# Column-tiled matmuls of linear attention gathered into every second step

## The chip, the cores and the metric

The program runs on one core of one Trainium2 chip. Time is device microseconds of one execution; a kernel's figure is the median of its runs. One more execution is recorded by the hardware profiler, and all rows below come from it. The engines are TensorE (PE, its weight loads as PEld), VectorE (DVE), ScalarE (ACT), GpSimd (POOL) and SyncE (SP), which issues most of the DMAs. Each engine works through its own instructions in order; a semaphore holds an instruction until what it needs is done.

## The reference

Linear attention over 8 batches of 8 heads, 576 tokens and 64 dimensions, then a mixture of 8 experts with one expert per token, and a second MLP:

```python
def phi(x):
    proj = np.einsum('bhsd,df->bhsf', x, w_phi)          # 64 -> 128 features
    proj = proj - np.max(np.abs(proj), axis=-1, keepdims=True)
    return np.concatenate([np.exp(proj), np.exp(-proj)], axis=-1)
q_p, k_p = (phi(q), phi(k))
kv = np.einsum('bhsf,bhsd->bhfd', k_p, v)
z = np.sum(k_p, axis=2)
num = np.einsum('bhsf,bhfd->bhsd', q_p, kv)
den = np.einsum('bhsf,bhf->bhs', q_p, z)[..., None] + 1e-06
attn = num / den
...
e_idx = np.argmax(logits, axis=1)                        # logits = x @ w_gate + bias of the modality
out[mask] = gate_w[mask, None] * (relu(x[mask] @ w1[e]) @ w2[e])
...
h = x @ w_in                                             # softmax times h, layer norm, then @ w_out
```

## The kernel before

Only attention is touched, the first third of the program. A unit (`ui`, 0 to 7) is two batches and four heads; the batches are its two halves. Its tokens are nine jobs `i`: 0 to 3 in half 0, 4 with a rest of both halves, 5 to 8 in half 1. A **step** `st` does one k job and one q job. The loop over the steps writes TensorE's order by hand (`manual_schedule`); the orders of the other engines follow from a timeline that the framework keeps while the program is built.

In step `st` TensorE gets, one behind the other:

- four transposes of k and q for the next step (`s0`, L255); ScalarE copies them into `hi` (L258), VectorE writes the remainder `lo` (L259);
- the projection of k, six matmuls (L267 to L269) into a bank `mm`; VectorE takes the largest absolute value (L271) and subtracts it (L273), and ScalarE writes the exponentials `e` (L277, L278);
- four transposes of the q features of the step two before (L330), which ScalarE turns into `qp` (L338), and an item of the list "f";
- the projection of q, in the same way, and up to two items "f";
- the sums over keys and values of the k job of two steps before (`accum_kv`, L283), four matmuls with 64 columns, into the bank `kv`. GpSimd adds the same `e` into `es` (L322);
- up to two items of the list "64": value groups (`num_part`, L440), 64 columns; and one of the list "32": row sums (`den_part`, L454) or sums of keys (`z_sum`, L384), 32 columns.

After jobs 4 and 8 `finish_kv` is called: ScalarE copies `kv` into `kt` (L325), and the items of that half are put on the lists: `kf_part` (L399, copied by L403 and L407), `z_part` (L416), four value groups, two row sums, and `finish`, which transposes the results back (L545, L560; VectorE L549 to L551 and L562) and, in odd units, does the gating (L575 to L626). An item runs when those before it are done.

PSUM has eight banks: three `tp` for transposes, four `mm` for projections, value groups, row sums and sums of keys, and one `kv`:

```python
tps = ctx.enter_context(tc.tile_pool(name="a_tp", bufs=3, space=PSUM))
mmp = ctx.enter_context(tc.tile_pool(name="a_mm", bufs=4, space=PSUM))
kvp = ctx.enter_context(tc.tile_pool(name="a_kv", bufs=1, space=PSUM))
```

In unit 5 the gating of the last part ends with `early.pick`: it finds the largest expert so far and writes its number into `ea_tab` (L845 to L857). In step 63 + `PRE` `prefetch` puts the loads of that expert's weights on SP's queue; they wait for `ea_tab` (issue at L884). In step 63 + `STEP0` `split_raw` cuts the first of these weights in two, with a cast on ScalarE (L926) and a subtraction on VectorE (L927), which write `w64`. L658 is the first matmul that reads prefetched weights.

Of the kernel before, what the change touches and what calls it, by code (L numbers as in the profile page):

```python
# [39 lines left out]
COLS64 = 2  # L40
COLS32 = 1
# [1 line left out]
BIAS = 8  # L43
BGN = 1
BGP = 100
PRE = 2
FSTEP = 2
RING = 5
RING0 = 1
# [144 lines left out]
def attention(ctx, tc, c, cnt, xe, q, k, v, ld, early, m, late):  # L194
# [86 lines left out]
    def accum_kv(u, i, e):  # L281
        def mm(half, h, lhsT, rhs, first, last):
            T.matmul(  # L283
                u.kv[half][(h % 2) * D : (h % 2 + 1) * D, h // 2, :], lhsT=lhsT, rhs=rhs,
                start=first, stop=last, skip_group_check=True,
            )

        def begin(half):
            u.kv[half] = kvp.tile([P, 2, 2 * F], F32, name="kv")
            u.es[half] = w2p.tile([P, 4, 2, F], F32, name="es")  # L290
            G.memset(u.es[half], 0.0)

        def rest(half, e, first, last):
            rows = slice(half * D, (half + 1) * D)
            es = u.es[half]
            for h in range(4):
                mm(half, h, u.src["v", 2][rows, h, :], e[rows, h], first and h < 2, last)
            G.tensor_tensor(out=es[rows], in0=es[rows], in1=e[rows], op=ALU.add)

        if i == 4:  # L300
            rest(0, e, False, True)
            u.erest = e
        else:
            half = i // 5
            if i in (0, 5):
                begin(half)
            if i == 5:
                rest(1, u.erest, True, False)
            rp, hp = (i - half) // 2 % 2, (i - half) % 2
            vt = u.src["v", half]  # L310
            for r in range(2):
                for h2 in range(2):
                    h = 2 * hp + h2
                    mm(
                        half, h, vt[:, h, (2 * rp + r) * D : (2 * rp + r + 1) * D], e[:, 2 * h2 + r],
                        i == 0 and r == 0, i == 8,
                    )
            es = u.es[half]
            ev = e.rearrange("p (h r) a f -> p h r (a f)", r=2)
            eo = es[:, 2 * hp : 2 * hp + 2].rearrange("p h a f -> p h (a f)")  # L320
            for r in range(2):
                G.tensor_tensor(out=eo, in0=eo, in1=ev[:, :, r, :], op=ALU.add)  # L322
        if i in (4, 8):
            u.kt[i // 5] = w2p.tile([P, 2, 2 * F], F32, name="kt")
            A.copy(u.kt[i // 5], u.kv[i // 5])  # L325
# [32 lines left out]
    def run_items(kind, count):  # L358
        ran = 0
        while ran < count:  # L360
            it = next((x for x in items if x.kind == kind and x.runnable()), None)
            if it is None:
                break
            if isinstance(it, Chain):
                said = next(it.gen, items)
                if said is not items:
                    if said:
                        until = step[0] + said[1]
                        it.kind, it.ready = said[0], lambda: step[0] >= until
                    ran += 1  # L370
                    continue
            else:
                it.fn()
            it.done = True
            items.remove(it)
            ran += 1
        return ran
# [3 lines left out]
    def z_sum(u, half):  # L381
        zp = mmp.tile([P, 2 * F], F32, name="mm")
        for h in range(4):
            T.matmul(  # L384
                zp[32 * h : 32 * h + 32, :], lhsT=c.ones32, rhs=u.es[half][:, h, :, :],
                start=True, stop=True, tile_position=(0, 32 * h), skip_group_check=True,
            )
        zs = w2p.tile([P, 2, F], F32, name="zs")
        A.copy(zs, zp.rearrange("p (a f) -> p a f", a=2))
        u.zs[half] = zs  # L390
# [21 lines left out]
    def z_part(u, half):  # L412
        gdt = gd[(2 * u.g + half) % 2]
        tp = tps.tile([P, 2, P], F32, name="tp")
        for fh in range(2):
            T.transpose(tp[:, fh, :], u.zs[half][:, fh, :], c.ident)  # L416
        A.copy(gdt[:, :, :, E : E + 1], tp.rearrange("p a (h n) -> p a h n", n=32)[:, :, :, 0:1])
# [50 lines left out]
    def finish_kv(u, half):  # L468
        at = step[0]
        zi = Item("32", lambda: z_sum(u, half), ready=lambda: step[0] > at)  # L470
        kfs = [Item("f", lambda j=j: kf_part(u, half, j)) for j in range(2)]
        zt = Item("f", lambda: z_part(u, half), after=[zi])
        begin = Item("0", lambda: outputs(u, half))
        parts = []
        for ci, (_, need) in enumerate(CHUNKS[half]):
            ok = lambda need=need: u.qdone.issuperset(need)
            for j in range(2):
                parts.append(Item("64", lambda ci=ci, j=j: num_part(u, half, ci, j), after=[begin, kfs[j]], ready=ok))
            parts.append(Item("32", lambda ci=ci: den_part(u, half, ci), after=[begin, zt, *kfs], ready=ok))

        def rest():
            yield from finish(u, half, 0, 4)
            if half == 1:
                yield from finish(u, 2, 0, 1)
            if u.g == 1:
                yield "0", 0
                yield from gating(u, 4 * half, 4 + half)
                if u.p2 == 2 and half == 1:
                    early.pick(cnt[0])
                    early.ready = True  # L490

        Chain("f", rest(), after=parts)

    def finish_last(u):
        z_sum(u, 1)
        yield
        for j in range(2):
            kf_part(u, 1, j)
        yield
        z_part(u, 1)  # L500
        yield
        outputs(u, 1)
        for ci in range(2):
            for j in range(2):
                num_part(u, 1, ci, j)
                yield
            den_part(u, 1, ci)
            yield
            if ci == 0:
                yield from finish(u, 2, 0, 1)  # L510
            else:
                yield from pend
            yield from finish(u, 1, 2 * ci, 2)
            if ci == 0:
                pend = gating(u, 4, 3)
                next(pend)
            else:
                pend = gating(u, 7, 2)
                for n in range(2):
                    for _ in range(FSTEP):  # L520
                        next(pend, None)
                    first_slot(n)
                yield from pend
# [142 lines left out]
    def last_unit():  # L666
        return U.get(len(units) - 1)
# [10 lines left out]
    n = len(steps)  # L678
    feats = {}
    bias = late()  # L680
    tail = []
    for st in range(n + LAGF):
        step[0] = st
        if st == 9 * 7 + PRE:
            assert early.ready
            m.prefetch()
        if st == 9 * 7 + STEP0:
            for i in range(RING0):
                m.split_raw(1, i)
        if st == BIAS:  # L690
            bias()
        run_items("0", 4)
        if st + 1 < n:
            ui, jobs = steps[st + 1]
            if ("k", 5) in jobs:
                unit(ui + 1)
            hl[st + 1] = s0(unit(ui), jobs)
        old = feats.pop(st - LAGF, ())
        u_old = unit(steps[st - LAGF][0]) if st >= LAGF else None
        kjobs = [(i, x) for kind, i, x in old if kind == "k"]  # L700
        qjobs = [(i, x) for kind, i, x in old if kind == "q"]
        if st < n:
            h_ = hl.pop(st)
            feats[st] = []
        for a in range(2):
            if st < n:
                kind, i = steps[st][1][a]
                feats[st].append((kind, i, proj(h_, a, kind)))
            if qjobs:
                i, x = qjobs.pop(0)  # L710
                q_features(u_old, i, x)
                u_old.qdone.add(i)
            run_items("f", FSLOT[a])
        for i, x in kjobs:
            accum_kv(u_old, i, x)
            if i in (4, 8):
                if i == 8 and u_old is last_unit():
                    tail.append(finish_last(u_old))
                else:
                    finish_kv(u_old, i // 5)  # L720
        run_items("0", 4)
        run_items("64", COLS64)
        run_items("32", COLS32)
        if st >= n and tail:
            for _ in range(TAIL):
                next(tail[0], None)
# [894 lines left out]
```

## Time and profile before

| what | value |
|---|---|
| median of 3 runs | 1294.19 us (1291.05 to 1295.75) |
| profiled execution | 1293.31 us, of which the span of the trace is 1291.6 us |
| TensorE, VectorE, ScalarE, GpSimd busy | 98%, 67%, 52%, 31% of the span |
| granted TensorE clock, mean | 0.996 of full speed |

The median is what the change is measured by; sums over the trace belong to the profiled execution, 0.88 us under the median. Matmuls overlap and their ends are modelled, so their start times tell more than their busy time. Start times are in us from the start of the span.

### The profile page before, as it was taken

What the parts mean: (1) busy time and instruction counts of PE and PEld (TensorE: products, weight loads), DVE (VectorE), ACT (ScalarE), POOL (GpSimd) and SP (SyncE); (2) the same over time, 40 slices, a digit from 0 to 9 for tenths busy, and PEclk for the clock granted to TensorE, in tenths of its full rate; (3) what the DMA queues carried; (4) which work ended last, traced back from release to release, by engine and by line L of the source; (5) the groups of instructions that cost most, each with busy time, mean ns of one, the idle gap of its engine ahead of it and who ended that gap; (6) DMA issues with size and microseconds to landing.
All of it is one profiled execution on the core that took longest, in us unless ns stands there. A gap on an engine that the chain in (4) does not pass through costs nothing.

```text
span 1291.6 us, 25365 instructions
## 1 busy us (share of the span) xinstructions
PE 1260.4 (98%) x9242; PEld 1057.8 (82%) x9242; DVE 869.3 (67%) x1620; ACT 666.8 (52%) x1254; POOL 403.8 (31%) x479
## 2 busy tenths in 40 slices
PE   8999999999999989999999999999999999999997
PEld 7767777777766889999999999987777778888885
DVE  8757866876775848778878787747555555566562
ACT  5666666666665426555555555534334434444442
POOL 6655674674663200000000000013323323333331
PEclk9999999999999999999999999999999999999999
DMA  8711342232132222222623132477877875566542
GB/s 246 214 54 58 107 133 58 87 117 85 50 116 67 91 67 92 67 83 66 197 66 83 51 83 67 130 213 192 233 204 168 248 169 142 137 153 139 145 121 57
DMA packets 273760, 156.78 MB, mean 121 GB/s; under 512 B 181824, under 2 KB 255712, under 8 KB 273632
## 3 DMA queue, kind: packets, MB, share of 16 engines
q1 hardware_dynamic: 267648, 136.01, 39.3%
q0 software_dynamic: 5824, 19.04, 3.8%
q8 instruction: 75, 1.23, 0.4%
q14 instruction: 53, 0.43, 0.1%
q10 hardware_dynamic: 160, 0.07, 0.0%
HBM read 166.67 MB, written 51.37 MB: 169 GB/s over the span
## 4 chain that ended last, share of the span: by engine, by line
PE 53%; DMA 5%; SPq 2%; issue 1%; ACT 1%; DVE 1%; POOL 0%; POOLq 0%; ACTq 0%; DVEq 0%
PE tp L1078 26%; PE h L1078 25%; DMA turned<-whi 2%; PE tp L898 1%; DMA gd<-xe 1%; SPq L1248 1%; DMA wlo<-turned 1%; PE tp L1389 1%; SPq L884 1%; DMA yin<-yd 0%; ACT ex L1265 0%; DVE ex L1270 0%; DMA xin<-xe 0%; ACT whi L1297 0%; SPq L1228 0%
## 5 line engine op out<-in xcount | busy, mean ns | idle before, releaser
L322 POOL TENSOR_TENSOR es<-es,e 128x512 f32<-128x512 f32 x128 | 163.8, 1286 | 102.5 <-ACT e L278 90.9
L927 POOL TENSOR_TENSOR yTl<-yin,yTh 128x512 fp32r<-128x512 f32 x36 | 46.8, 1300 | 443.2 <-ACT yTh L926 442.1
L1078 PE MATMUL tp<-xTh,whi 128*128 128x256 f32 x432 | 121.7, 282 | 2.5 <-PEq L1470 2.1
L1078 PE MATMUL h<-hTl,whi 128*128 128x256 f32 x432 | 120.6, 279 | 0.4 <-DVE hTl L1093 0.4
L1078 PE MATMUL tp<-xTh,wlo 128*128 128x256 f32 x432 | 120.6, 279 | 0.0
L1078 PE MATMUL tp<-xTl,whi 128*128 128x256 f32 x432 | 120.5, 279 | 0.0
L1078 PE MATMUL h<-hTh,whi 128*128 128x256 f32 x432 | 120.5, 279 | 0.0
L1078 PE MATMUL h<-hTh,wlo 128*128 128x256 f32 x432 | 120.5, 279 | 0.0
L271 DVE TENSOR_REDUCE m<-mm 128x4 f32<-128x512 f32 x144 | 97.1, 681 | 15.9 <-PE mm L269 15.9
L259 DVE TENSOR_TENSOR lo<-tp,hi 128x512 fp32r<-128x512 f32 x72 | 49.6, 689 | 82.5 <-ACT hi L258 82.0
L1265 ACT ACTIVATE ex<-h,s_mx,gt 128x1024 f32<-128x1024 f32 x36 | 43.4, 1207 | 111.6 <-issue 56.8
L1260 DVE TENSOR_REDUCE s_mx<-h 128x1 f32<-128x512 f32 x72 | 46.3, 685 | 80.6 <-PE h L1078 80.6
L267 PE MATMUL mm<-wphi_hi,hi 128*128 128x256 f32 x288 | 94.2, 327 | 1.0 <-ACT hi L258 1.0
L1275 ACT ACTIVATE sq<-ex 128x1024 bf16<-128x1024 f32 x36 | 38.1, 1058 | 97.9 <-DVE ex L1272 97.9
L1078 PEld LDWEIGHTS tp<-xTh,whi 128*128 128x128 f32 x432 | 81.3, 188 | 2.9 <-issue 2.2
L338 ACT ACTIVATE qp<-tp 128x512 f32<-128x512 f32 x128 | 69.3, 597 | 25.8 <-PE tp L330 22.7
L1078 PEld LDWEIGHTS tp<-xTh,wlo 128*128 128x128 f32 x432 | 81.9, 190 | 0.0
L1078 PEld LDWEIGHTS h<-hTh,wlo 128*128 128x128 f32 x432 | 81.9, 190 | 0.0
L268 PE MATMUL mm<-wphi_lo,hi 128*128 128x256 f32 x288 | 81.6, 283 | 0.0
L1078 PEld LDWEIGHTS h<-hTl,whi 128*128 128x128 f32 x432 | 81.1, 188 | 0.6 <-DVE hTl L1093 0.6
L269 PE MATMUL mm<-wphi_hi,lo 128*128 128x256 f32 x288 | 81.4, 283 | 0.0
L1078 PEld LDWEIGHTS h<-hTh,whi 128*128 128x128 f32 x432 | 81.3, 188 | 0.0
(427 smaller groups left out, 3818.9 us busy)
## 6 DMA issues: line engine op xcount, KB each, us to landing
ldk<-in_moe_w_dram SPq DMA_DIRECT2D x66, 512.0 KB
ldv<-in_moe_w_dram SPq DMA_DIRECT2D x66, 512.0 KB
ldq<-in_moe_w_dram SPq DMA_DIRECT2D x44, 512.0 KB
turned<-whi SPq DMA_DIRECT2D x35, 512.0 KB
wlo<-turned SPq DMA_DIRECT2D x140, 128.0 KB
yd<-yo SPq DMA_DIRECT2D x36, 256.0 KB
yin<-yd SPq DMA_DIRECT2D x18, 512.0 KB
xin<-xe SPq DMA_DIRECT2D x16, 512.0 KB
```

The lines of the kernel that those rows point to most:

```text
L259: V.tensor_tensor(out=lo, in0=tp, in1=hi.bitcast(F32), op=ALU.subtract)
L267: T.matmul(o, lhsT=hi[:, 2 * a + j, :], rhs=c.wphi_hi, start=(j == 0), stop=False, skip_group_check=True)
L268: T.matmul(o, lhsT=hi[:, 2 * a + j, :], rhs=c.wphi_lo, start=False, stop=False, skip_group_check=True)
L269: T.matmul(o, lhsT=lo[:, 2 * a + j, :], rhs=c.wphi_hi, start=False, stop=True, skip_group_check=True)
L271: V.tensor_reduce(out=m, in_=pj, axis=AX.X, op=ALU.max, apply_absolute_value=True)
L322: G.tensor_tensor(out=eo, in0=eo, in1=ev[:, :, r, :], op=ALU.add)
L338: A.activation(u.qp[half][:, fh, 2 * hp : 2 * hp + 2, o : o + 2 * P], tp.rearrange("p (h r) t -> p h (r t)", r=2), AF.Exp, scale=sc,)
L927: eng.tensor_tensor(out=lo, in0=src, in1=hi.bitcast(F32), op=ALU.subtract)
L1078: T.matmul(o, lhsT=l, rhs=r, start=first and n == 0, stop=last and n == 2, skip_group_check=True)
L1260: V.tensor_reduce(out=mx, in_=h[:, sl], axis=AX.X, op=ALU.max, negate=True)
L1265: A.activation(ex, h, AF.Exp, bias=mx, scale=g, accum_out=sm)
L1275: A.activation(sq, ex, AF.Square, accum_out=var)
```

## The change

The sums of keys and values of a step are put on a list. In odd steps, and from the last one on, the list is worked off: after each of its jobs come up to two items "64", four in all, and behind them up to two items "32". In even steps TensorE has only matmuls that use all 128 columns. `PRE` goes from 2 to 4, so that the prefetch stands behind `early.pick` in the new order. Below `finish_kv` nothing is changed, nor is any pool.

```diff
-PRE = 2
+PRE = 4
...
-    tail = []
+    tail, sums = [], []
...
-        for i, x in kjobs:
-            accum_kv(u_old, i, x)
-            if i in (4, 8):
-                if i == 8 and u_old is last_unit():
-                    tail.append(finish_last(u_old))
-                else:
-                    finish_kv(u_old, i // 5)
-        run_items("0", 4)
-        run_items("64", COLS64)
-        run_items("32", COLS32)
+        sums.extend((u_old, i, x) for i, x in kjobs)
+        if st % 2 or st >= n - 1:
+            more = COLS64 * 2
+            while sums or more:
+                if sums:
+                    us, i, x = sums.pop(0)
+                    accum_kv(us, i, x)
+                    if i in (4, 8):
+                        if i == 8 and us is last_unit():
+                            tail.append(finish_last(us))
+                        else:
+                            finish_kv(us, i // 5)
+                run_items("0", 4)
+                run_items("64", min(more, COLS64))
+                more -= min(more, COLS64)
+            run_items("32", 2 * COLS32)
```

The first place is TensorE's order at the change from unit 0 to unit 1. `ldv` is v, `kv_658` and `kv_952` are tiles in the one `kv` bank; a number is only the tile's. Before:

```order
L283 MATMUL kv_658<-e_722,ldv_232 64x256 x4
L255 MATMUL tp_899<-ident_88,ldk_435 128x128 x2
...
L560 MATMUL tp_946<-ident_88,num0_602 128x128 x4
L283 MATMUL kv_952<-e_797,ldv_437 64x256 x4
L384 MATMUL mm_961<-es_659,ones32_109 32x256 x4
L255 MATMUL tp_968<-ident_88,ldrk_441 128x128 x2
```

And in the changed kernel:

```order
L269 MATMUL mm_885<-wphi_hi_97,lo_816 128x256
L283 MATMUL kv_647<-e_692,ldv_232 64x256 x4
L283 MATMUL kv_906<-e_744,ldv_437 64x256 x4
L454 MATMUL mm_915<-qp_236,gd0_208 32x256 x8
L454 MATMUL mm_925<-qp_236,gd0_208 32x320 x8
L255 MATMUL tp_936<-ident_88,ldrk_441 128x128 x2
```

The 128-column part of a step stood between the last sums of the old unit and the first of the new; now nothing does, and the row sums that read `qp_236` come after both. The same holds in units 0, 2, 4 and 6 between jobs 4 and 5: eight places in all.

The second place is VectorE's order where `ea_tab` is written, in the steps after unit 6's end. `w64` is what `split_raw` writes. Before:

```order
L271 TENSOR_REDUCE m_5194<-mm_5187 128x4
L259 TENSOR_TENSOR lo_5184<-tp_5178,hi_5183 128x512
L857 CAST ea_tab_178<-ea_res_177 128x2
L562 TENSOR_TENSOR xt4_5106<-tp_5208,r_5115 128x2x256
L273 TENSOR_TENSOR xsk_5196<-mm_5187,m_5194 128x512
L271 TENSOR_REDUCE m_5221<-mm_5214 128x4
L562 TENSOR_TENSOR xt4_5106<-tp_5225,r_5115 128x2x256
...
L273 TENSOR_TENSOR xsq_5292<-mm_5283,m_5290 128x512
L927 TENSOR_TENSOR w64_5467<-ldk_5158,w64_5466 128x1024
L259 TENSOR_TENSOR lo_5340<-tp_5334,hi_5339 128x512
```

And in the changed kernel (its lines are numbered six higher here):

```order
L273 TENSOR_TENSOR xsq_5105<-mm_5096,m_5103 128x512
L618 TENSOR_TENSOR g_base_5147<-g_rk_5088,g_base_5147 128x8 x4
...
L863 CAST ea_tab_178<-ea_res_177 128x2
L271 TENSOR_REDUCE m_5193<-mm_5186 128x4
L273 TENSOR_TENSOR xsk_5195<-mm_5186,m_5193 128x512
L259 TENSOR_TENSOR lo_5183<-tp_5177,hi_5182 128x512
...
L271 TENSOR_REDUCE m_5296<-mm_5289 128x4
L933 TENSOR_TENSOR w64_5427<-ldk_5260,w64_5426 128x1024
L259 TENSOR_TENSOR lo_5286<-tp_5280,hi_5285 128x512
```

`ea_tab` stood ahead of nearly two steps of projections before the split; now it stands ahead of one, and the small operations of its chain follow each other.

The third place is ScalarE's order at the same split. Before:

```order
L403 COPY kf_5277<-tp_5278 128x2x128
L407 COPY gd1_209<-tp_5278 128x2x2x8
L926 CAST w64_5466<-ldk_5158 128x1024
L277 ACTIVATE e_5267<-xsk_5265 128x4x128
L278 ACTIVATE e_5267<-xsk_5265 128x4x128
```

And in the changed kernel:

```order
L403 COPY kf_5231<-tp_5237 128x2x128
L407 COPY gd1_209<-tp_5237 128x2x2x8
L932 CAST w64_5426<-ldk_5260 128x1024
L258 CAST hi_5285<-tp_5280 128x512
L338 ACTIVATE qp_4571<-tp_5303 128x2x256
```

Behind the cast now stands the `hi` of the next step, where the exponentials of k stood.

## Rows read from the trace of the kernel before

**Rows 1.** The page, engines: busy us (share of the span) xinstructions.

```profile
PE 1260.4 (98%) x9242; PEld 1057.8 (82%) x9242; DVE 869.3 (67%) x1620; ACT 666.8 (52%) x1254; POOL 403.8 (31%) x479
```

**Rows 2.** One stretch: us, busy us (xinstructions) by engine, PEclk, DMA share, GB/s.

```profile
200.00:300.00 100.00, 99.22 (x882) 72.80 (x870) 73.81 (x155) 65.72 (x156) 61.68 (x57) 1.00 0.31 96
```

**Rows 3.** Waits of TensorE, 33 to 410 us: us in total, times, longest.

```profile
PE tp L560 <- DVE lo L259: 1.9, 6, 0.3
PE tp L560 <- DVE gs L551: 0.7, 1, 0.7
PE mm L440 <- ACT kf L403: 0.4, 1, 0.4
```

**Rows 4.** Timeline of TensorE, one step: start, us, line, out<-in, tile and count.

```profile
381.14 0.28 PE L268 MATMUL mm<-wphi_lo,hi 128*128 128x256 f32 x1
381.25 0.28 PE L269 MATMUL mm<-wphi_hi,lo 128*128 128x256 f32 x1
381.46 1.08 PE L283 MATMUL kv<-e,ldv 128*64 128x256 f32 x8
382.37 1.90 PE L440 MATMUL mm<-qp,kf 128*64 128x256 f32 x16
384.20 1.07 PE L454 MATMUL mm<-qp,gd 128*32 128x256 f32 x16
385.20 0.66 PE L255 MATMUL tp<-ident,ldk 128*128 128x128 f32 x4
```

**Rows 5.** TensorE's groups by shape, 33 to 400 us: busy us, mean ns.

```profile
L440 PE MATMUL mm<-qp,kf 128*64 128x256 f32 x230 | 28.4, 379 | 0.0
```

**Rows 6.** Timeline of TensorE and ScalarE at the copy of `kv`.

```profile
392.87 1.08 PE L283 MATMUL kv<-e,ldrv 64*64 64x256 f32 x8
...
394.00 0.59 ACT L325 COPY kt<-kv 128x512 f32<-128x512 f32 x1 [0.39 <-PE kv L283]
```

**Rows 7.** Timeline where TensorE waits for ScalarE.

```profile
421.06 0.21 ACT L425 COPY den<-mm 128x64 f32<-128x64 f32 x1 [0.75 <-PE mm L454]
...
421.32 0.33 PE L545 MATMUL tp<-ident,den 128*128 128x128 f32 x1 [0.33 <-ACT den L425]
```

**Rows 8.** Timelines of VectorE, SyncE and ScalarE at the prefetch.

```profile
360.29 0.76 DVE L618 TENSOR_TENSOR g_base<-g_rk,g_base 128x8 f32<-128x8 f32 x4
...
368.16 0.15 DVE L857 CAST ea_tab<-ea_res 128x2 int32<-128x2 f32 x1
...
370.10 0.41 SPq L884 DMA_DIRECT2D ldk<-in_moe_w_dram  x1
...
372.20 1.09 ACT L338 ACTIVATE qp<-tp 128x512 f32<-128x512 f32 x2 [0.49 <-PE tp L330]
...
374.19 1.04 ACT L926 CAST w<-ldk 128x1024 fp32r<-128x1024 f32 x1 [0.55 <-DMA ldk<-in_moe_w_dram]
```

**Rows 9.** Timeline of TensorE, end of the step that begins at 385.20.

```profile
388.07 1.08 PE L283 MATMUL kv<-e,ldv 128*64 128x256 f32 x8
```

**Rows 10.** Line L927 in the whole span: ns min/median/max, first and last start.

```profile
L927 DVE TENSOR_TENSOR w<-ldk,w x10: 1216/1225/3836, 375.3 to 792.1; 128x1024 fp32r<-128x1024 f32 x10
```

**Rows 11.** Timeline of TensorE at the first prefetched weights.

```profile
428.86 1.89 PE L658 MATMUL mm<-ldk,xsk 128*128 128x256 f32 x8
```

**Rows 12.** Timeline of VectorE in a stretch with gating.

```profile
235.05 0.68 DVE L273 TENSOR_TENSOR xsk<-mm,m 128x512 f32<-128x512 f32 x1
235.65 0.68 DVE L562 TENSOR_TENSOR xt<-tp,r 128x512 f32<-128x512 f32 x1
...
244.11 1.31 DVE L583 SCALAR_TENSOR_TENSOR g_first<-g_L,rev 128x40 f32<-128x40 f32 x1
```

**Rows 13.** Stretches around a wait of TensorE in the expert stage; columns as in rows 2.

```profile
473.50:477.30 3.80, 1.65 (x15) 1.41 (x13) 2.91 (x3) 2.71 (x5) 0.00 (x0) 1.00 0.49 139
478.20:481.60 3.40, 3.40 (x19) 3.40 (x17) 0.00 (x0) 0.00 (x0) 0.00 (x0) 0.50 0.40 47
485.50:496.40 10.90, 10.90 (x98) 10.90 (x98) 9.01 (x13) 7.28 (x10) 0.00 (x0) 1.00 0.29 90
```

## The prediction

> **What bounds the kernel now.** I read the summary first: TensorE is busy for 98% of the span and no other engine passes 67% [rows 1]. That share is an average, so the second view is the table by stage: from 200 to 300 us TensorE is busy 99.2 of 100 us at the full granted clock, VectorE 73.8, ScalarE 65.7, GpSimd 61.7 [rows 2]. The third is who TensorE waits for between 33 and 410 us: 3.0 us in all, in eight waits [rows 3]. So attention is as long as TensorE's own order makes it. A microsecond taken from that order shortens the kernel; every microsecond that TensorE is made to wait lengthens it. The other engines have a quarter of each step to spare, but only as far as the banks between them and TensorE let them use it.
>
> **What the change removes: changes of shape.** One step now goes from matmuls that use all 128 columns to 64-column ones, often on to 32-column ones, and back. What that costs is in the start times. L268 to L269 is 381.14 to 381.25, 0.11 us; L269 to the first 64-column L283, at 381.46, is 0.21: 0.10 more [rows 4]. The 16 L440 last 1.90 us in eight pairs, one matmul of them 0.38 [rows 4, 5]; so the pairs start (1.90 - 0.38) / 7 = 0.22 apart, the last at 383.89, and the first L454 comes at 384.20, 0.31 later: 0.09 more. I take 0.095 us for every change of shape, the way back included. Counted along the two orders, there are 200 such changes in the program before and 119 in the changed one; 81 x 0.095 = **7.7 us saved**. The number of matmuls stays.
>
> The Trainium skill says in TensorEngine Tiling (Array Packing), Key Properties, that a change of tiling mode drains the TensorE. If the drain were all that is left of the last matmul, 0.38 - 0.22 = 0.16 to 0.17 us, 81 of them would be 13.5 us; the rows show a little over half of it.
>
> **What it adds, first: waits for the one bank of sums.** The pool of `kv` has one bank. Now the copy L325 that empties it, after job 4 or 8, has a step before the next sums begin. In the changed order eight places have the last sums of one half and the first of the next back to back, with nothing between (the first piece of order shows one). TensorE then waits for: the end of its last matmul, 0.38 after that one's start; ScalarE's start, 394.00 against an end of 392.87 + 1.08 = 393.95, 0.05; the copy, 0.59 [rows 6]; and the way back, where a copy ends at 421.06 + 0.21 = 421.27 and L545, which waited for it, starts at 421.32, 0.05 [rows 7]. That is 1.07 from start to start, where the next pair would have come after 0.22: 0.85 us each, **8 x 0.85 = 6.8 us**. It can hardly be less, each part being a row. It is more where ScalarE is still in a pair of exponentials (1.09 for two [rows 8]): up to 8 x 1.1 = 9 us on top. I take the low end, because in the new order the exponentials ahead of L325 belong to the step before. The Trainium skill says in Perfetto Trace Analysis, Optimization Strategy, that the same gap repeated on the engine that should be saturated can mean too few PSUM buffers; no such gap is in this trace yet, and these waits would be one.
>
> **Second: the first load of expert weights.** It starts when `ea_tab` is written and lands 6.0 us later: 368.16, issue at 370.10, and at 374.19 ScalarE's cast L926, after 0.55 of waiting [rows 8]. Job 8's gating is one step later now, so `ea_tab` is; in VectorE's new order its chain, which ran from 360.29 to 368.16 among other work [rows 8], stands in one piece, about 4 us by its durations. In the new ScalarE order the cast stands right behind the two copies of `kf` of the same step. I count from that step's first transpose. The batch before it began 5.0 us earlier (two groups of sums at 0.9 [rows 4], a wait of 0.85, row sums of 1.0 [rows 4] and some 1.2); VectorE is through with that step's projections about 2.1 after the batch began; so `ea_tab` is written at 2.1 + 4.1 - 5.0 = 1.2, the load lands at 7.2, and ScalarE reaches the cast at about 4.3 (2.87 for the step [rows 4, 9], then the transposes and copies of `kf`). It stands still for 2.9 us with the next step's `hi` behind it. The cast takes 1.04 [rows 8]; the split on VectorE 1.22 where GpSimd is quiet, as it would be here with ScalarE's exponentials held up, 3.84 beside its adds [rows 10]; `lo` 0.6: 10.2 with the latencies. TensorE needs that `lo` for its third `tp` tile from there, at about 6.5: 3.7, and 0.4 for a transpose of `kt` held by an earlier `lo`, **4 us once**. Bounds: 0.5 if the load is as early as now, 7 if the split takes 3.84. The two steps on `PRE` cost nothing for the other loads: L658 reads them from 428.86 on [rows 11], 50 us after.
>
> **Third: VectorE gets its work in other portions.** It has five large operations for a step, two L271, two L273, one L259, 0.60 us from start to start [rows 12]: 3.0. Two steps with only 128-column work pass on TensorE in about 2 x 2.87 us (385.20 to 388.07 [rows 4, 9]); with the operations of `finish` VectorE has 8 us to do in them, with gating 10 to 11 (L583 alone 1.31 [rows 12]). The batch behind gives it time: two kv groups of 0.9 and four value groups of 0.9 to 1.1, so that the fourth value group, which needs the bank of this step's q projection, is not reached before some 11 us. I charge nothing for the `mm` banks. What remains are the three `tp` banks: a transpose of `finish` waits for the `lo` three tiles back. Today that and `gs` are 1.9 + 0.7 us [rows 3]. By the same walk it is 0.4 in three plain stretches and 1 to 1.5 in the six with gating, 8 us: **5 more than now**, with bounds of 0 and 10.
>
> **Fourth:** at the four changes of unit where `qp` is still to be read by the row sums, now the last thing in the batch, the exponentials of q (1.09) come after it, and TensorE's next q transposes wait 0.3 for them: **1 us in all** (0 to 3).
>
> GpSimd's adds are released by ScalarE's exponentials, not by TensorE's order; they cost nothing while GpSimd idles a third of the stage [rows 2]. In the tail only jobs 5 and 6 move, one step on, work that TensorE does anyway: 0.
>
> **Sum.** -7.7 + 6.8 + 4 + 5 + 1 = +9.1 us. The profiled execution took 1293.31, so 1302.4; the median of the runs shown is 0.9 above it: **1303 us**.
>
> **Rivals.**
> *A wash.* The kv waits are as priced, but VectorE keeps up and the load is waited for 0.5: -7.7 + 6.8 + 0.5 + 1 = +0.6, 1295 us. For it speaks that TensorE waits only 3.0 us now; against it that two 128-column steps in a row are shorter than VectorE's work in them.
> *Worse.* ScalarE is in its exponentials at half of the kv copies, +4.5; the waits for `lo` are at their upper bound, +5; and the long wait at the weights lowers TensorE's clock. After a stretch in which it was busy for 1.65 of 3.8 us, the granted clock was 0.50, the lower level of 1.2 GHz, for 3.4 us, in which 19 matmuls ran, where 98 take 10.90 at full clock [rows 13]: 19 x 0.11 = 2.1, so +1.3. That makes 1314 us.
> *Faster.* Each change of shape costs the whole drain, 0.17, where nothing overlaps it, and the other terms are nothing: 13.8 - 6.8 = 7 us gained, 1287 us. It decides from (6.8 + 6.5) / 81 = 0.164 us for a change; the rows show 0.095 at two kinds of change.
> That the change does not do what it says is excluded by the order.
>
> **Chances.** A change of 0.5%, 6.5 us, is about what a measurement of this kernel can tell from none. Forecast 0.44, worse 0.13, wash 0.35, faster 0.08. The forecast's own span is 1299 to 1309, the wash's 1288 to 1300.7. Slower by over 0.5%, above 1300.7, holds the worse case and nearly all of the forecast's: 0.55; within 0.5% the rest of the two: 0.37; faster: 0.08. The range for 8 in 10 cuts off half of the worse case, most of the faster one and the low end of the wash: 1291 to 1314.
>
> **What would show it.** In the profile after: as many matmuls as now; the 0.21 from L269 to L283 in half as many places; among TensorE's waits eight for the copy of `kt`, 0.7 to 0.9 each; one of 3 to 6 us where the cast of `w64` is, with ScalarE waiting for a load in front of it; L560 or L399 behind `lo` for 5 to 10 us. It would be wrong if the kv waits are far from 0.85, or if TensorE waits for `mm` banks in the value batches, which I price at nothing.

## The result, and the profile after

The changed kernel took 1307.05 us (median of 4 runs, 1305.44 to 1310.26), the kernel before 1293.87 beside it (4 runs): a ratio of 1.0108, with a 95% interval of 1.0090 to 1.0126. It is 13.2 us slower. The profiled execution took 1310.26 us with a span of 1308.6, so it is the slowest of the four and 17.0 us longer in its span than that of before; its single terms add up to that, not to 13.2.

The whole loss lies in attention. The first L658, after attention's end, starts at 428.86 us before [rows 11] and at 446.43 after, 17.6 later; from there to the end of the span it is 862.7 and 862.1 us.

The page's row of TensorE, and the stretch from 200 to 300 us, which answer to [rows 1, 2]:

```profile
PE 1255.8 (96%) x9242; PEld 1062.8 (81%) x9242; DVE 868.8 (66%) x1620; ACT 662.6 (51%) x1254; POOL 404.3 (31%) x479
...
200.00:300.00 100.00, 95.75 (x863) 71.57 (x859) 71.89 (x149) 63.40 (x154) 60.99 (x56) 1.00 0.29 93
```

The number of matmuls is the same. But in 100 us of the steady stretch TensorE starts 863 where it did 882: it is now idle for 4 of 100 us. For whom, the waits of TensorE from 33 to 410 us say (in total, times, longest), against 3.0 us in [rows 3]:

```profile
PE kv L283 <- ACT kt L325: 5.6, 8, 0.8
PE tp L399 <- DVE lo L259: 4.4, 3, 1.5
PE tp L560 <- ACT qp L338: 3.2, 1, 3.2
PE tp L255 <- ACT gd L407: 2.8, 4, 0.9
PE tp L560 <- DVE gs L551: 1.6, 3, 0.5
PE tp L255 <- DMA ldk<-in_k_dram: 1.4, 1, 1.4
PE tp L255 <- DMA ldq<-in_q_dram: 1.1, 1, 1.1
PE tp L399 <- ACT qp L338: 0.8, 4, 0.2
PE tp L560 <- DVE lo L259: 0.7, 3, 0.2
```

These are four kinds: the `kv` bank (8 times), one long wait at the cast of `w64` (the 3.2), the first loads of unit 1, and the `tp` banks (the other five rows, 10.3 us). None is for an `mm` bank. The list ends at 410 us, where the changed kernel has attention's tail still ahead of it; that comes below. The view counts a wait from the modelled end of the last matmul; from start to start each is a little longer.

**The kv bank**, between job 4 and job 5 of unit 4, in the timeline:

```profile
244.97 1.08 PE L283 MATMUL kv<-e,ldrv 64*64 64x256 f32 x8
...
245.67 0.38 PE L283 MATMUL kv<-e,ldrv 64*64 64x256 f32 x2
...
246.10 0.58 ACT L325 COPY kt<-kv 128x512 f32<-128x512 f32 x1 [1.76 <-PE kv L283]
246.73 1.08 PE L283 MATMUL kv<-e,ldrv 64*64 64x256 f32 x8 [0.68 <-ACT kt L325]
```

The last pair of the first group starts at 245.67, the next one at 246.73: 1.06 to 1.07, where pairs otherwise follow at 0.22. So 0.85 us, and seven of the eight read alike to 0.01. The first, at 33.92, is 0.96: there ScalarE was still in the exponentials of q when the sums ended, and its copy starts 0.15 after them.

**The cast of w64**, in the timelines of VectorE, SyncE, ScalarE and TensorE, with the granted clock of the stretches around it:

```profile
380.04 0.17 DVE L863 CAST ea_tab<-ea_res 128x2 int32<-128x2 f32 x1
...
382.15 0.41 SPq L890 DMA_DIRECT2D ldk<-in_moe_w_dram  x1
...
386.74 1.04 ACT L932 CAST w<-ldk 128x1024 fp32r<-128x1024 f32 x1 [3.23 <-DMA ldk<-in_moe_w_dram]
387.69 0.58 ACT L258 CAST hi<-tp 128x512 fp32r<-128x512 f32 x1
...
388.17 1.09 ACT L338 ACTIVATE qp<-tp 128x512 f32<-128x512 f32 x2
...
389.31 1.12 PE L560 MATMUL tp<-ident,num 128*128 128x128 f32 x4 [3.22 <-ACT qp L338]
...
386.50:389.30 2.80, 0.00 (x0) 0.00 (x0) 1.48 (x2) 2.52 (x4) 2.72 (x3) 0.86 1.03 357
388.54:395.37 6.83, 6.06 (x26) 3.16 (x28) 4.22 (x7) 2.35 (x6) 4.29 (x4) 0.50 0.73 246
396.00:400.00 4.00, 4.00 (x42) 2.45 (x39) 0.00 (x0) 1.71 (x6) 0.70 (x1) 1.00 0.00 0
```

ScalarE stands still for 3.23 us in front of the load, with `hi` and the exponentials of q behind the cast; TensorE needs the bank that the exponentials free. The granted clock falls within the stretch without a matmul and is 0.50, the lower level of 1.2 GHz, from 388.54 to 395.37. The matmuls that start from 389.31 to 395.6 take 2.9 us more than the same ones at full clock, by their single starts.

**The first loads of unit 1**, which no row of before had shown:

```profile
34.93 1.08 PE L283 MATMUL kv<-e,ldv 128*64 128x256 f32 x8
37.38 0.44 PE L255 MATMUL tp<-ident,ldk 128*128 128x128 f32 x2 [1.36 <-DMA ldk<-in_k_dram]
38.87 0.44 PE L255 MATMUL tp<-ident,ldq 128*128 128x128 f32 x2 [1.05 <-DMA ldq<-in_q_dram]
```

Before, TensorE ran the same transposes without a wait:

```profile
38.90 0.44 PE L255 MATMUL tp<-ident,ldk 128*128 128x128 f32 x2
39.17 0.38 PE L255 MATMUL tp<-ident,ldq 128*128 128x128 f32 x2
```

Now the last pair of its batch starts at 35.6, and it comes to them some 3 us earlier.

**The tp banks**, two places that come back in every pair of units:

```profile
250.95 1.20 DVE L583 SCALAR_TENSOR_TENSOR g_first<-g_L,rev 128x40 f32<-128x40 f32 x1
252.08 0.68 DVE L259 TENSOR_TENSOR lo<-tp,hi 128x512 fp32r<-128x512 f32 x1
252.81 0.76 PE L399 MATMUL tp<-idwg,kt 128*128 128x144 f32 x4 [1.34 <-DVE lo L259]
...
299.61 0.61 ACT L278 ACTIVATE e<-xsk 128x512 f32<-128x512 f32 x1
300.13 0.35 ACT L403 COPY kf<-tp 128x256 f32<-128x256 f32 x1
300.38 0.19 ACT L407 COPY gd<-tp 128x32 f32<-128x32 f32 x1
300.62 0.44 PE L255 MATMUL tp<-ident,ldk 128*128 128x128 f32 x2 [0.88 <-ACT gd L407]
```

At the first, `lo` stands behind the gating on VectorE; at the second the two copies out of the bank stand behind the exponentials of k on ScalarE, and those behind VectorE's subtraction.

**The tail**, at the row sums of the last unit's first half, in the timelines of ScalarE and TensorE:

```profile
425.56 1.16 ACT L338 ACTIVATE qp<-tp 128x512 f32<-128x512 f32 x2
426.53 0.26 ACT L417 COPY gd<-tp 128x8 f32<-128x8 f32 x1
426.84 1.59 PE L454 MATMUL mm<-qp,gd 128*32 128x256 f32 x21 [1.77 <-ACT gd L417]
```

These row sums read `gd`, and its copy stands behind exponentials of q on ScalarE. From the last transpose to L454 it is 2.04 us where a change of shape without a wait takes 0.20, so 1.8. In the kernel before, that copy was done 3.5 us ahead of the row sums, and nothing waits there; the tail's other waits stand in both kernels.

**What was saved** is read from start times of single matmuls. Into 64 columns:

```profile
256.07 0.28 PE L269 MATMUL mm<-wphi_hi,lo 128*128 128x256 f32 x1
256.28 1.08 PE L283 MATMUL kv<-e,ldv 128*64 128x256 f32 x8
257.20 1.03 PE L440 MATMUL mm<-qp,kf 128*64 128x256 f32 x8
```

From L269 to the first pair it is 0.21 in place of 0.117, as in [rows 4]. But the four pairs of L283 then take 0.92 to the next group, where four steady pairs take 4 x 0.216 = 0.86: the second pair after a change is 0.05 late as well. (Behind each of the eight waits for the kv bank, where the shape stays, the second pair is as late: it goes with a stop of the engine, not with the change alone.) The median excess over steady spacing in both kernels, second start included, is 0.141 us into 64 columns, 0.157 back to 128, 0.124 from 64 to 32 and 0.170 from 32 to 128. By these and the counted kinds the 81 fewer changes save 11.9 us. A second reading, all spacings taken at their undisturbed medians, makes attention 10.2 us shorter.

The balance of the profiled pair, start to start: -10.2 for the order, +6.9 kv bank, +3.4 cast, +2.9 half clock behind it, +2.65 first loads, +10.6 `tp` banks (17.0 against 6.4, the four waits for `qp` included), +1.8 in the tail: +18.1 for the 17.6 between the two ends. The two readings of the order's term lie further apart than that difference.

### The profile page after: what moved, and what is told of

Same layout as the page of the kernel before. It is cut to its first block, busy times and chain, and to the rows that moved or that the text cites. A ratio compares the mean times of both kernels' runs of the same rounds, so it can differ in the third digit from the quotient of the medians.

```text
span 1308.6 us, 25370 instructions
## 1 busy us (share of the span) xinstructions
PE 1255.8 (96%) x9242; PEld 1062.8 (81%) x9242; DVE 868.8 (66%) x1620; ACT 662.6 (51%) x1254; POOL 404.3 (31%) x479
## 4 chain that ended last, share of the span: by engine, by line
PE 53%; DMA 5%; DVE 1%; SPq 1%; issue 1%; ACT 1%; POOL 0%; POOLq 0%; ACTq 0%; DVEq 0%
PE tp L1084 26%; PE h L1084 25%; DMA yin<-yd 2%; DMA turned<-whi 1%; PE tp L904 1%; DMA gd<-xe 1%; SPq L890 1%; PE tp L1395 1%; DMA xin<-xe 0%; SPq L1254 0%; ACT ex L1271 0%; DVE ex L1276 0%; DMA wlo<-turned 0%; DMA out_dram<-wab,gt 0%; DVE wlo L933 0%
## 5 line engine op out<-in xcount | busy, mean ns | idle before, releaser
L267 PE MATMUL mm<-wphi_hi,hi 128*128 128x256 f32 x288 | 93.9, 326 | 1.1 <-ACT hi L258 1.1
L1084 PEld LDWEIGHTS tp<-xTl,whi 128*128 128x128 f32 x432 | 82.2, 190 | 0.0
L269 PE MATMUL mm<-wphi_hi,lo 128*128 128x256 f32 x288 | 81.3, 282 | 0.0
```

The source lines that it names most:

```text
L267: T.matmul(o, lhsT=hi[:, 2 * a + j, :], rhs=c.wphi_hi, start=(j == 0), stop=False, skip_group_check=True)
L269: T.matmul(o, lhsT=lo[:, 2 * a + j, :], rhs=c.wphi_hi, start=False, stop=True, skip_group_check=True)
L1084: T.matmul(o, lhsT=l, rhs=r, start=first and n == 0, stop=last and n == 2, skip_group_check=True)
```

## The experiments

Chips differ: on the one that timed two of the kernels below, the kernel before took 1299.7 us, elsewhere 1293. So each ratio is to the kernel before on the same chip; "end" is the start of the first L658 in the profiled execution, where attention is over. One execution of each kernel is profiled, and some of these lie at an end of their kernel's range; so an end tells where that execution lost time, and the median is the kernel's time.

| run | median, us | ratio (95%) | end, us |
|---|---|---|---|
| before | 1293.87 | 1 | 428.86 |
| changed | 1307.05 | 1.0108 (1.0090 to 1.0126) | 446.43 |
| later split | 1308.77 | 1.0110 (1.0086 to 1.0134) | 449.32 |
| halves | 1301.77 | 1.0062 (1.0041 to 1.0082) | 440.90 |
| four tp | 1305.54 | 1.0088 (1.0065 to 1.0111) | 441.57 |
| rows only | 1293.22 | 0.9995 (0.9981 to 1.0009) | 429.45 |
| fixed cast | 1303.42 | 1.0076 (1.0058 to 1.0094) | 444.08 |
| + early loads | 1301.29 | 1.0069 (1.0050 to 1.0088) | 438.62 |
| + halves | 1292.45 | 1.0000 (0.9986 to 1.0014) | 428.20 |
| + four tp | 1284.36 | 0.9940 (0.9917 to 0.9962) | 420.80 |
| before + loads, four tp | 1293.56 | 0.9946 (0.9928 to 0.9965) | 428.75 |
| before, batch split | 1327.51 | 1.0203 (1.0169 to 1.0237) | 461.68 |
| "+ four tp", again | 1284.41 | 0.9927 (0.9905 to 0.9949) | 424.52 |
| before + loads, four tp, again | 1288.46 | 0.9963 (0.9949 to 0.9977) | 425.23 |

**Later split.**

```diff
-STEP0 = 6
+STEP0 = 8
```

> The changed kernel with the first split of expert weights (the cast of w64) two steps later (STEP0 6 to 8), nothing else. Theory (the changed kernel is slower by the waits that its trace shows, each of them on the path): the wait at the cast, 3.5 us of TensorE, and the 2.4 us of half clock behind it both go, since the load lands a step before the cast: 1307.1 - 5.9 = 1301.2 us, and TensorE's longest wait in attention is under 2 us. Rival (VectorE is behind with its work anyway, and a wait taken away comes back at the next transposes): 1305 to 1307 us.

The time did not move, and the trace says why: the edit did nothing. The same wait stands at the same place.

```profile
391.07 1.05 ACT L932 CAST w<-ldk 128x1024 fp32r<-128x1024 f32 x1 [3.36 <-DMA ldk<-in_moe_w_dram]
```

ScalarE's order is not that of the code: the framework's timeline put the cast at the same point though it was called two steps later, presumably where it takes the weights to have landed, and that is some 3 us before they do. So neither theory was tried here. In this execution unit 1's loads were waited for 4.5 us, and the clock was down from 35 to 45 us.

**Halves**, on the kernel with the later split:

```diff
-        if st % 2 or st >= n - 1:
+        if any(i in (1, 3, 4, 6, 8) for _, i, _ in sums) or st >= n - 1:
```

> The changed kernel with the later split and with batches that end with a half: TensorE gets its column-tiled work behind the k jobs 1, 3, 4, 6 and 8 of a unit in place of every odd step, so a step without sums always lies between the copy of kv and the next sums in that bank. Theory (the eight waits for the one kv bank are 0.85 us each, as their start times show, and are on the path): against the kernel with the later split alone -6.8 us, +1.0 for seven more changes of shape, 5.8 us faster, about 1295.4 us; no wait for the copy of kt. Rival (the eight waits only give VectorE and ScalarE time that they need, so the waits for tp banks grow by as much): within 1.5 us of the kernel with the later split alone, the waits for tp at 20 us in place of 14.

It gave 7.0 us. The eight waits for `kt` are gone, and those for `tp` did not grow by as much; the cast still held TensorE, now for 2.9 us at L330. But more had changed in this execution: unit 1's loads were waited for 2.1 us in place of 4.5, and the wait in the tail is gone. Whether the waits for the kv bank were on the path is told better below, where the loads and the cast no longer wait.

**Four tp**, on the kernel with the later split:

```diff
-    tps = ctx.enter_context(tc.tile_pool(name="a_tp", bufs=3, space=PSUM))
-    mmp = ctx.enter_context(tc.tile_pool(name="a_mm", bufs=4, space=PSUM))
+    tps = ctx.enter_context(tc.tile_pool(name="a_tp", bufs=4, space=PSUM))
+    mmp = ctx.enter_context(tc.tile_pool(name="a_mm", bufs=3, space=PSUM))
```

> The changed kernel with the later split and with four tp banks and three mm banks in place of three and four. Theory (the rest of the loss are transposes that wait for a tp bank, 14 us of TensorE in attention in the changed kernel against 5 before, because VectorE's lo and ScalarE's copies of kf come late in two steps that hold only 128-column work): with a fourth bank most of it goes, 6 to 9 us faster than the kernel with the later split alone, 1292 to 1295 us. Rival (VectorE's and ScalarE's work is what is late, and the mm bank that was given up is missed at once): the waits move to L267 and L440, and the time is the same or longer, 1301 to 1310 us.

3.2 us faster, which the two intervals do not tell from nothing; the waits tell more. Those for `tp` fell under 2 us, and these came, from 33 to 410 us:

```profile
PE mm L267 <- ACT num L427: 4.0, 3, 1.3
PE mm L440 <- DVE xsk L273: 3.5, 3, 1.2
PE mm L267 <- DVE xsq L273: 2.7, 6, 0.5
PE mm L440 <- ACT num L427: 1.1, 1, 1.1
```

The rival fits in this order: the work of VectorE and ScalarE comes late, and the bank chooses who shows it.

**Rows only**, on the kernel before:

```diff
-PRE = 2
+PRE = 4
...
-STEP0 = 6
+STEP0 = 8
...
-        run_items("32", COLS32)
+        if st % 2 or st >= n - 1:
+            run_items("32", 2 * COLS32)
```

> The kernel before, with one part of the change: only the 32-column items (row sums and sums of keys) run in every second step, two at a time; sums of keys and values and value groups stay in every step. The prefetch is two steps later and the split too, as gating ends later. 15 changes of shape fewer than before (185 against 200), no back-to-back use of the kv bank. Theory (a change of shape costs 0.147 us, the longer second start behind it included, as the start times of both kernels show): 2.2 us faster than before, 1291.7 us, and no new wait. By the 0.095 of the prediction: 1.4 us faster. Rival (whatever holds work back a step makes transposes wait for tp banks): 1296 us or more, with L560 and L399 waiting 3 us more than before.

No difference. At undisturbed spacing its attention is 2.4 us shorter than before, as 15 changes at 0.147 said; its disturbances are some 3 us longer, 1.4 of them at unit 1's first loads and 1.4 at L399. A small gain and a small loss, both seen in the trace, not in the time.

**Fixed cast**, the later split with ScalarE's order pinned:

```diff
-        self.tc.nc.scalar.copy(hi, src)
+        cast = self.tc.nc.scalar.copy(hi, src)
+        if src is self.raw[0] and self.nsplit == 1:
+            self.tc.keep_in_program_order(cast)
```

> The changed kernel with the first split called two steps later and its cast fixed in ScalarE's order behind what was issued before it. (The kernel with only the call two steps later left the cast where it was in ScalarE's order, so the same wait of 3.3 us stood in its trace; here 34 more instructions of ScalarE stand ahead of it.) Theory (the wait at the cast and the half clock behind it are on the path): no wait of TensorE over 2 us from 360 us on, the full clock up to 420 us, 5.9 us faster than the changed kernel, 1301.2 us. Rival (VectorE is behind and the wait comes back at the next transposes): 1305 to 1308 us.

The wait of 3.2 us is gone from the list, the rest of which reads as in the changed kernel, and the clock is full from 360 to 420 us. By the ratios, 1.0110 to 1.0076, that is 4.4 us; 5.9 were expected, within what the intervals allow. The wait did not come back. In the profiled execution the clock fell further on, behind the wait in the tail: it is 0.50 from 422.98 to 426.39, and the 32 row sums there take 3.84 us, where the next kernel, with the same wait and the full clock, runs them in 2.15.

**Early loads**, on top:

```diff
     unit(0)
+    unit(1)
     zero = w1p.tile([P, ROW], F32, name="zero")
```

> The kernel with the fixed cast, and the loads of unit 1 put on SP's queue ahead of the zero fill of xe and of the 16 small loads of the modality ids, which they followed. Theory (in the changed kernel TensorE comes to unit 1's first transposes 1.5 us earlier than before and waits 2.65 us there for k and q, and in some executions the clock falls to half behind it, while the kernel before arrives as they land): no wait of L255 for a load at 35 to 40 us, 2.6 us faster than with the fixed cast alone if the clock held there, up to 6 if not: 1295 to 1298.6 us. Rival (the zero fill and the small loads are then what is late, or the time is used up at the next wait): within 1 us of the fixed cast alone.

TensorE no longer waits for unit 1's loads. The time is inconclusive: 0.9 us by the ratios. The profiled executions differ by 5.5 us at attention's end, but the one without this edit is the slowest of seven, with the clock at 0.72 from 38 to 44 us and at half in the tail, and the one with it the fastest of six.

**Halves on top of both.**

> The kernel with the fixed cast and the early loads, and batches that end with a half (behind the k jobs 1, 3, 4, 6 and 8). Theory (eight waits of 0.85 us for the kv bank are on the path, seven more changes of shape cost 1.0): 5.8 us faster than the kernel with the fixed cast and the early loads, 1289 to 1293 us. Rival (the waits for tp banks take it up): within 1.5 us of that kernel. The earlier run with such batches was 7.0 us faster than the one without, with the two other waits still in it and the half clock for some 10 us at 38 us.

8.9 us by the ratios, more than the theory's 5.8 though hardly beyond the intervals, and level with the kernel before. These waits are left up to 410 us:

```profile
PE tp L560 <- DVE lo L259: 6.5, 12, 0.7
PE tp L255 <- DVE xt L562: 2.2, 6, 0.4
PE tp L255 <- DVE lo L259: 1.4, 1, 1.4
PE tp L416 <- ACT qp L338: 0.2, 1, 0.2
```

So the eight waits for the kv bank were on the path: in neither of the two profiled executions do the loads or the cast wait or the clock fall in attention, and its end is 10.4 us earlier. Of that the kv bank is 6.9, less 1.0 for seven more changes; the wait of 1.8 in the tail, which the theory did not know, is gone too, and start to start the `tp` waits are between 1 and 2 us shorter. The row on the copies of `kf` and `gd`, 2.8 us, is gone from the list.

**Four tp on top.**

> The same with four tp banks and three mm banks. Theory (what is left are waits for tp banks): 3 us faster than the kernel with three, as between the two earlier kernels with and without the fourth bank, 1286 to 1290 us, below the kernel before. Rival (with batches every second step four value groups and two row sums want mm banks at once, and waits for mm take the place of those for tp): the same time or up to 4 us longer.

7.8 us by the ratios, below the kernel before. Here the fourth bank helps and the one given up is little missed: the waits for `mm` banks at L267 that came are 4.0 us in two rows, of which the larger is

```profile
PE mm L267 <- DVE xsq L273: 3.3, 6, 0.7
```

**The same edits without the order.**

> The kernel before, its order untouched, with two of the edits that were put on the changed kernel: unit 1's loads early on SP's queue, and four tp and three mm banks. It tells how much of a gain over the kernel before is owed to these and how much to the order of the column-tiled work. Theory (before, TensorE waits 3 us for tp banks and not at all for unit 1's loads, so both edits have little to take): 1290 to 1294 us, so that most of the 8.5 us by which the kernel with batches ended at the halves, fixed cast, early loads and four tp banks beat the kernel before comes from its order. Rival (the banks are what helps, in any order): 1286 us or less.

0.9946, as good as the one above, but on another chip, on which the kernel before itself is 6 us slower. So the two were timed side by side.

> The kernel with batches that end with a half, fixed cast, early loads and four tp banks once more, on one chip with the next one. Until now the two were timed on different chips, on one of which the kernel before took 1299.7 us. Theory (the order of the column-tiled work is worth something once its waits are gone: in the traces attention's last matmul starts at 419.3 us with it, at 427.3 with the two edits on the old order): 8 us below the kernel before with early loads and four tp banks. Rival (the two edits are the whole gain, since both kernels came out at 0.994 of the kernel before beside them): within 2 us of it.

> The kernel before with early loads and four tp banks, on one chip with the one above. Theory: it gains only where the kernel before waits for unit 1's loads on that chip: 1290 to 1294 us, 8 us above the kernel above. Rival: the same time as the kernel above.

Neither theory holds. The two edits are worth 5 us to the old order, and the new order 4.05 us beyond them (1284.41 against 1288.46; the intervals of the two ratios just touch, and each of the 6 executions of the new order is below each of the 12 of the old). The ends differ by 0.7 only: the execution of the new order that was profiled is its slowest, with the clock at 0.50 from 52.6 to 56.0 us. The stretch from 200 to 300 us, first of the old order with the edits, then of the new one, shows both parts:

```profile
200.00:300.00 100.00, 100.00 (x889) 74.00 (x887) 75.21 (x157) 67.21 (x160) 62.03 (x57) 1.00 0.31 96
...
200.00:300.00 100.00, 98.74 (x897) 75.47 (x899) 78.33 (x157) 66.56 (x161) 63.03 (x58) 1.00 0.30 96
```

With four `tp` banks the old order does not wait in this stretch and starts 889 matmuls where it did 882 [rows 2]; the new order is idle for 1.3 us and still starts 897. On the other chip the old order with the same edits had L399 wait 2.5 us for `lo`, three times, so what the edits give it differs between executions.

**Batch split**, on the kernel before: the sums ahead of the projection of q.

```diff
         for a in range(2):
+            if a:
+                for i, x in kjobs:
+                    accum_kv(u_old, i, x)
...
         for i, x in kjobs:
-            accum_kv(u_old, i, x)
             if i in (4, 8):
```

> The kernel before with the sums of keys and values placed ahead of the projection of q instead of behind it, so that 128-column work splits the column-tiled work of a step in two: 274 changes of shape in place of 200, the same matmuls, finish_kv called where it was. Theory (a change costs the late first start and the longer second one behind it: 0.141 us into 64 columns, 0.157 back to 128, 0.124 from 64 to 32, 0.17 from 32 to 128; the 74 more are mostly of the first two kinds): 11 us slower than before, 1304 us. By the 0.095 of the prediction: 7 us slower, 1300 us. Rival (the drain is hidden where the engine has other work queued): within 3 us of before.

The time is 27.8 us longer, more than all three said, but the trace splits it: at undisturbed spacing attention is 11.9 us longer, 0.16 for each of the 74 changes, so the price of a change is settled well above 0.095. The rest are new waits and 3.4 us at half clock from 146.1 on. These two waits are the most:

```profile
PE tp L560 <- ACT qp L338: 7.1, 6, 1.2
PE mm L440 <- ACT kf L403: 5.0, 11, 1.1
```

## Why the prediction was right, point by point

It forecast slower, at 1303 with a range of 1291 to 1314; it was 1307. The sum was +9.1 where the profiled pair shows +17.6 and the medians +13.2, and no term had the wrong sign. That the number came within 4 us is in part luck: three costs, 7.4 us together, were left at nothing, the `tp` banks were short by 4.6, and against them stand 2.5 to 4.2 us that the order saved beyond its term.

- *Changes of shape, 7.7 us saved.* The step was mis-sized: 10.2 to 11.9. It priced the first late start alone, 0.095; the start after it is late as well, and a change is 0.12 to 0.17. But it is not one delay: 0.09 to 0.11 at the first start and 0.02 to 0.06 at the second. The rule that a change drains the TensorE, cited from the Trainium skill (TensorEngine Tiling (Array Packing), Key Properties), gave 0.16 to 0.17 by the prediction's reading of the drain, and that is nearer to the measured mean of 0.147 than the 0.095 taken from the rows. The *faster* rival's price was thus nearly true, but it needed the other terms to be nothing.
- *The kv bank, 8 x 0.85.* Seven waits of 0.85 us, to the hundredth, and one of 0.96, the only one at which ScalarE was still in its exponentials. The kernel with halves on top of the fixed cast and the early loads shows that they were on the path. The rule cited from the Trainium skill (Perfetto Trace Analysis, Optimization Strategy), that a repeated gap on the engine that should be saturated can mean too few PSUM buffers, fits the five rows on `tp` as well as the one on `kv`: a fourth `tp` bank helped beside batches that end with the halves. With the later split it moved the waits to the `mm` banks, and in the old order it came together with the early loads.
- *The load of the weights, 4 us.* The mechanism and the place were right: `ea_tab`, the load 6.7 us behind it, ScalarE 3.23 in front of it, TensorE 3.5 from start to start, 3.4 of it waiting. It named the bank as held by `lo`; the trace names the exponentials of q, which stand behind the same cast. The clock was left to the *worse* rival at 1.3; it fell, and cost 2.9. Fixing the cast took back 4.4.
- *VectorE in other portions, 5 us.* Mis-sized by half: with the next item 10.6 from start to start, where the two had 6, and 7.3 in the list of waits; that is at the upper bound, which the *worse* rival took. The gating in front of `lo` was foreseen (5.1 in the two `lo` rows); that ScalarE's copies of `kf` come late for the same reason, 2.8, was not. That nothing waits for `mm` banks held with four of them, and no longer with three.
- *qp at four changes of unit, 1 us.* Four waits, 0.8.
- *The tail, 0.* It was put at nothing as work that TensorE does anyway; its row sums came to wait 1.8 us for a copy on ScalarE.
- *Not foreseen:* unit 1's first loads, 2.65 us and in some executions a low clock behind it. TensorE arrived there some 3 us earlier, ahead of loads that had been in time before.

What stays open: why the executions of one kernel differ by 3 to 14 us (the batch split 1319.89 to 1334.24, the kernel before beside the first experiments 1290.34 to 1301.2). The wait for the first loads and the clock behind it differ among the profiled ones, but those that were only timed have no trace. Nor is it shown what of the 5 us that the two edits give the old order belongs to which, nor why the kernel before was slower on one chip.

## What to carry to other kernels

Gathering work of one kind into every second turn saves its changes, but its producers and its bank then see two turns of demand in one: before such a change, look for every buffer that is refilled back to back and for every load that now just arrives in time. A gain of this sort shows only when the waits that it makes are cured as well; here that took four more edits, and two of them, the early loads and the fourth `tp` bank, were worth 5 us to the old order as well. And an edit to the code is no edit to an engine's order until that order is seen to have changed.

## What the runs showed of the hardware

The second start after a change of tile shape is late too: 0.267 us from the first 64-column pair to the second, 0.216 after that; 0.165 between the first two transposes after a 32- or 64-column stretch, 0.109 after that. Behind the eight waits for the kv bank, where the shape stays, it is 0.267 as well. In a stretch of 3.2 us without a matmul the granted clock fell to 0.50, for 6.8 us, in 6.06 of which TensorE was busy with 26 matmuls. Around the waits for unit 1's loads it went either way: full in the changed kernel (waits of 1.4 and 1.1 us), 0.72 from 38 to 44 us with the fixed cast (1.4 and 1.2), and 0.50 from 36 to 42 with the later split (3.3 and 1.2). So it did behind the wait of 1.77 us in the tail: full in the changed kernel and with the early loads, 0.50 with the fixed cast.
